# Attention and experts on one core: GpSimd's operations of a pair put beside VectorE's six stretches of maxima

## The chip, the cores and the metric

One Trainium2 chip, one of its cores. The metric is the device time of one execution in microseconds (us); the time of a kernel is the median of its runs. Engines are named as the profile names them: PE is TensorE (PEld its weight loads), DVE is VectorE, ACT is ScalarE, POOL is GpSimd, SP is the engine whose queue issues most transfers.

## What is computed

Attention over 8 batches of 8 heads with pooled queries, and on its output a mixture of 8 experts, one expert for each token:

```python
# attention: q, k, v are (8, 8, 1152, 64)
q_pool = q.reshape(B, H, S // 2, 2, D).mean(axis=3)
scores = scale * q_pool @ k^T
attn = exp(scores - max(scores)) / (sum + 1e-09)
x = attn @ v                                   # 4608 tokens of 512
# experts
logits = x @ w_gate + modality_bias[modality_id]
e = argmax(logits);  g = softmax(logits)[e]
out = g * (relu(x @ w1[e]) @ w2[e])
```

## The kernel before

**Pairs and steps.** The 64 heads go in 32 pairs: head j of two batches lies on partitions 64j to 64j+63. Work on a pair is written as 18 steps (`NSTEP`), and a loop over all steps (line 1250) writes PE's, ACT's, DVE's and POOL's instructions in the order in which they stand in the program; each engine then runs its own in that order and waits for semaphores. SP's transfers are not in this order by hand: a scheduler places them where it expects their data to be ready. Tables of step numbers (`T_SPLIT`, `T_QH`, `T_LO`, `T_HD`, `T_VH`, `T_VL`, `T_VS`, `XL`, lines 41 to 95) say at which step, counted from the pair's first, an operation is written; a negative number lies in earlier pairs' steps, so that while one pair's scores run, the next pairs' operands are made.

**What a step has.** PE makes scores into three PSUM banks (`psc`, lines 990 and 991); ACT turns a bank into exponentials (`Pe`, line 992); the exponential is kept as two float16 parts, the upper half read in place and the lower half (`Pl`) scaled by ACT (line 973, 1152 columns) or by DVE (line 975, 576 columns, uint16 to float16). PE then multiplies both with the values (`xp`, lines 1050 to 1052) into the banks X0 (first head) and X1 (second head). When a head is done, DVE scales its result into `x2` (lines 1068 to 1073); ACT and DVE then split x2 into two float16 parts (`split_x` line 1009, `split_xl` line 1019).

**The maxima.** The softmax's row maxima of a later pair are found from an approximate product of queries and keys (`event`, line 907): six events of a pair, at the steps of `EVENTS` (line 161), that is at 13, 16, 1, 4, 7 and 10 of the running 18 steps. In each, PE writes the banks M0, M1, M2 and, for four of them, X0 or X1 (lines 919 to 933), and DVE reduces them (line 915). Four events have two reductions of 512 columns and one of 1024; the one at step 4 (`rest`) has two small ones, the one at step 13 (`block4`) one of 1024. DVE's lower half of every third step stands just ahead of each event's reductions, so that DVE goes through six stretches in a pair: lower half, maxima, then whatever the tables put behind them, then the next lower half. After the event at step 10 the maxima are gathered (`row`: `m9` line 855, a transpose on PE line 859, `mr` line 868) and a transfer writes `mr` into B2's last row (line 869), which the scores of the next pair need.

**POOL's operations of a pair**, for the pairs from the fourth on (above `HELD`): the pooled sum of the queries (`rawq`, line 700), its float16 copy (`qh`, line 709), the low part of the queries (`lo<-rawq,qh`) and of the keys in two halves (`lo<-rawk,hi`, line 745), the high part of the values in two pieces (`VH`, line 835, 640 and 512 columns), a small copy (`both`, line 814), and the issue of the transfer that loads the keys as float16 (`hi`, line 721). DVE makes the low part of the values in two pieces (`vl`, line 831) and the shifted values (`VS`, line 847).

**Waits set by hand.** `hold(this, until)` (line 659) adds a wait between two instructions; the reason that stands beside it is that the two would share a port. `fast[0]` is the last lower half that was written for DVE. Before, these wait for `fast[0]`: the pooled sum, `lo`'s second index (the first half of the keys) and the second piece of `VH`. `lo`'s first index (the queries) waits for the first `vl` of the pair before it.

**Side work.** After every eighth pair a generator (`route`, line 298) ranks 1152 tokens; it runs a few instructions at a time in the steps of `QUIET`, and its matrix products (lines 353 and 355) take a PSUM bank from `some` (line 642) and wait while `held` says so (line 644).

Of the kernel before, what the change touches and what calls it, by code (L numbers as in the profile page):

```python
# [30 lines left out]
SQ = S // 2  # L31
# [10 lines left out]
HELD = 2  # L42
# [8 lines left out]
LAG = 3  # L51
XL = (6, 5, 3)
LD = 1
# [13 lines left out]
T_KQ = -46  # L67
T_SPLIT = -34
T_QH = -33
T_HI = (-29, -24)  # L70
BY_DMA = 3
T_HD = -33
T_LO = (-23, -26, -17, -19, -26, -17, -23)
T_MAX = -24
# [5 lines left out]
LAG0 = 7  # L80
T_SQ = -20
T_POW = -18
T_VH = (-14, -15)
T_VL = (-11, -2)
T_VS = -12
PARTS = ((0, 5, 9), (0, 5, 9))
# [78 lines left out]
FD = 0  # L165
PD = 0
MANUAL = {ET.PE, ET.Activation, ET.DVE, ET.Pool}
# [444 lines left out]
def attention(tc, ctx, att, ident, npairs, xpool, on_two, on_split, on_scale, jobs, side, set_pm, started, ahead, hip):  # L612
# [28 lines left out]
    bank = lambda: banks[next(turns3)]  # L641
    some = lambda: banks[X0 if now[0] % NSTEP in (13, 14, 15) else M2] if by_events() else bank()
    apart = lambda: banks[M2] if by_events() else bank()
    set_pm(some, lambda: by_events() and now[0] % NSTEP not in (2, 3, 13, 14, 15))

# [10 lines left out]
    st = {p: {} for p in range(npairs)}  # L656
    vl_first, fast = {}, [None]

# [45 lines left out]
    def split_qh(p):  # L704
        s = st[p]
        qh = s["qh"]
        made.add((p, "qh"))
        if p > 1:
            (nc.gpsimd if QH_POOL else nc.vector).tensor_copy(qh, s["q"][:, 0:SQ])
        else:  # L710
            nc.scalar.copy(qh, s["q"][:, 0:SQ])
        for j in range(2):
            r = slice(j * D, (j + 1) * D)
            cols = slice(j * SQ, (j + 1) * SQ) if p < BY_HEADS else slice(4 * P + j * D, 4 * P + (j + 1) * D)
            move(QB[p % 2].rearrange("p u n -> p (u n)")[r, cols], qh[r, cols.start - j * SQ:cols.stop - j * SQ])
# [15 lines left out]
    def split_lo(p, i):  # L731
# [13 lines left out]
        done = (nc.gpsimd if p < 2 or i in LO_POOL else nc.vector).tensor_tensor(o[:, r], t[:, r], h[:, r], op=ALU.subtract)  # L745
        if p > HELD and i < 2:
            hold(done, fast[0] if i else vl_first.pop(p - 1))

# [46 lines left out]
    def power(p):  # L795

        s = st[p]
        pt = some()
        nc.tensor.matmul(pt[:, 0:1], ones.broadcast_to([P, P]), s["ss"], start=True, stop=True)
        later_end(PD if p else 0, lambda: scales(p, pt))  # L800

# [16 lines left out]
    def values(p, i, lo):  # L818
# [8 lines left out]
        if lo and p < 2:  # L827
            nc.gpsimd.tensor_scalar(v, v, s["sc"], None, op0=ALU.mult)
            nc.gpsimd.tensor_tensor(flat(s["vl"][:, c]), v, vh, op=ALU.subtract)
        elif lo:  # L830
            done = nc.vector.scalar_tensor_tensor(flat(s["vl"][:, c]), v, s["sc"], vh, op0=ALU.mult, op1=ALU.subtract)  # L831
            if i == 0:
                vl_first[p] = done
        elif p > 1 and i in VH_POOL:
            done = nc.gpsimd.tensor_scalar(vh, v, s["sc"], None, op0=ALU.mult)  # L835
            if p > HELD and i:
                hold(done, fast[0])
        else:
            nc.scalar.activation(vh, v, AF.Copy, scale=s["sc"])
# [354 lines left out]
    for p in range(npairs):  # L1194
        b = NSTEP * p
        go = lambda t, f, *a, p=p, b=b, **k: at(b + t, p, lambda: f(p, *a), **k)
        if p > 1:
            d = D2 if p == 2 else (0,) * 5
            go(T_K2 - b if p == 2 else T_KQ, load_kq, end=False)
            go(T_SPLIT + d[0], split_q)  # L1200
            go(T_QH + d[1], split_qh)
            if p < BY_DMA:
                for i in range(2):
                    go(T_HI[i] + d[2], split_hi, i)
            else:
                go(T_HD, load_hi)
            for i in range(3 if LOC else 7):
                go(T_LO[LOCI[i] if LOC else i] + d[3], split_lo, i)
            if p < BY_HEADS:
# [6 lines left out]
        elif p:  # L1216
            go(T_P1 - b, place, end=False)
            go(T_M1 - b, lambda p: mxq.append(maxpass(p)), end=False)
            go(T_LV, load_v)
        sq, power_, vh, vs, vl = (T_SQ, T_POW, T_VH, T_VS, T_VL) if p > 1 else V1 if p else V0  # L1220
        if p == 1:
# [547 lines left out]
```

## Time and profile before

| what | value |
|---|---|
| median of 3 runs | 1179.87 us (1179.81 to 1183.86) |
| the profiled execution's own time | 1182.24 us |
| its span, first to last instruction | 1180.5 us |
| mean granted TensorE clock | 0.992 |
| stage of the attention's pairs | from about 30 to 790 us |
| stage of the experts | from about 830 us to the end |

The profile has one execution. Busy time of an engine is the union of its instructions' times in a stretch. In the windows view each row is a stretch of the span with each engine's busy time and instruction count, the granted clock, the busy share of the DMA engines and GB/s. The timeline view has an instruction (or a run of like ones) per row, with the idle time ahead of it in square brackets and what ended that. The chain of waits goes back from the end of a stretch through what released each step.

### The profile page before, as it was taken

The page shows a single profiled execution, that of the slowest core. Times are in us where ns is not written, and L with a number is a line of the kernel's source. Part 1 is how long each engine was busy: PE and PEld are TensorE (multiplying, and loading weights), DVE is VectorE, ACT ScalarE, POOL GpSimd, SP SyncE. Part 2 cuts the span into 40 slices and gives each one's busy share as a digit, 9 for nine tenths or more (in the row PEclk, how much of TensorE's full clock was granted, in tenths as well). Part 3 has the DMA queues.
Part 4 walks back from the last instruction along what each step waited for, and adds up shares of the span by engine and source line. Part 5 has one row for each costly group of instructions (what it writes and reads, how often), then busy time and mean ns, then how long its engine had stood idle before and what let it go on. Part 6 is the DMA issues. An engine that isn't in the chain of part 4 may idle for free.

```text
span 1180.5 us, 36614 instructions
## 1 busy us (share of the span) xinstructions
PE 1100.3 (93%) x15060; PEld 781.2 (66%) x15060; DVE 990.5 (84%) x1730; ACT 894.6 (76%) x1403; POOL 439.1 (37%) x469
## 2 busy tenths in 40 slices
PE   7989898999889989889999998999999999999997
PEld 3766666666666666656666666786676676767665
DVE  6899989999989899979999999988798666675755
ACT  5988888888878888878888888877656566565654
POOL 6754444344443445334443454213223211212111
PEclk8999999999999999989999999999999999999999
DMA  7677868769677696775967766469899999999993
GB/s 218 165 202 179 170 153 184 183 149 203 149 158 175 148 188 162 177 158 134 194 160 180 168 150 147 108 204 294 256 271 267 322 288 280 270 278 274 281 277 118
DMA packets 179696, 237.41 MB, mean 201 GB/s; under 512 B 96479, under 2 KB 127215, under 8 KB 179520
## 3 DMA queue, kind: packets, MB, share of 16 engines
q1 hardware_dynamic: 169254, 206.65, 67.4%
q0 software_dynamic: 10256, 28.33, 11.0%
q8 instruction: 120, 1.97, 0.7%
q14 instruction: 56, 0.46, 0.1%
q10 hardware_dynamic: 10, 0.00, 0.0%
HBM read 163.22 MB, written 18.99 MB: 154 GB/s over the span
## 4 chain that ended last, share of the span: by engine, by line
PE 47%; DVE 37%; DMA 5%; ACT 5%; issue 4%; POOL 2%; POOLq 0%; SPq 0%; DVEq 0%
DVE mp L915 17%; DVE Pl L975 6%; PE po L1531 4%; PE po L1533 4%; PE po L1532 4%; PE ph L1424 4%; PE ph L1426 4%; PE ph L1425 4%; PE psc L991 4%; PE psc L990 4%; DMA B<-mr 4%; PE xp L1050 2%; DVE vl L831 2%; DVE x L1073 2%; DVE x L1019 2%
## 5 line engine op out<-in xcount | busy, mean ns | idle before, releaser
L992 ACT ACTIVATE Pe<-psc 128x432 int32<-128x432 f32 x768 | 383.1, 527 | 112.2 <-PE psc L991 98.1
L1050 PE MATMUL xp<-VH,Pe 128*128 128x65 f16 x2880 | 349.1, 194 | 0.0
L1052 PE MATMUL xp<-VS,Pl 128*128 128x65 f16 x2880 | 346.2, 193 | 0.8 <-DVE Pl L975 0.8
L1051 PE MATMUL xp<-vl,Pe 128*128 128x64 f16 x2880 | 345.6, 192 | 0.0
L1050 PEld LDWEIGHTS <-Pe 128*128 128x128 f16 x2880 | 267.0, 98 | 106.1 <-issue 61.1
L915 DVE TENSOR_REDUCE mp<-pm 128x2 f32<-128x1024 f32 (+3 forms) x319 | 297.1, 939 | 43.4 <-PE pm L933 25.8
L991 PE MATMUL psc<-B 65*128 65x432 f16 (+2 forms) x1152 | 304.4, 288 | 8.7 <-DMA B<-mr 8.6
L990 PE MATMUL psc<-B 128*128 128x432 f16 (+2 forms) x1152 | 305.0, 287 | 1.6 <-ACT Pe L992 0.5
L1051 PEld LDWEIGHTS <-Pe 128*128 128x128 f16 x2880 | 266.5, 98 | 44.7 <-issue 0.4
L1052 PEld LDWEIGHTS <-Pl 128*128 128x128 f16 x2880 | 265.0, 97 | 1.2 <-DVE Pl L975 1.2
L973 ACT ACTIVATE Pl<-Pe 128x1152 f16<-128x1152 uint16 x186 | 216.5, 1164 | 5.9
L1424 PE MATMUL ph<-xpart,w1h 128*128 128x256 f16 x544 | 148.3, 273 | 0.5 <-DVE hl L1430 0.5
L1426 PE MATMUL ph<-xpart,w1l 128*128 128x256 f16 x544 | 148.3, 273 | 0.0
L1425 PE MATMUL ph<-xpart,w1h 128*128 128x256 f16 x544 | 148.3, 273 | 0.0
L975 DVE TENSOR_SCALAR Pl<-Pe 128x576 f16<-128x576 uint16 (+1 forms) x198 | 132.9, 672 | 4.4 <-ACT Pe L992 3.4
L991 PEld LDWEIGHTS <-B 65*128 65x128 f16 x1152 | 113.1, 98 | 11.7 <-issue 1.3
L835 POOL TENSOR_SCALAR VH<-rawv,sc 128x512 f16<-128x512 f32 (+1 forms) x60 | 104.4, 1740 | 42.7 <-PE psc L991 29.1
L990 PEld LDWEIGHTS <-B 128*128 128x128 f16 x1152 | 111.8, 98 | 6.8 <-issue 1.4
L1430 DVE SCALAR_TENSOR_TENSOR hl<-ph,hh 128x512 f16<-128x512 f32 x72 | 49.6, 688 | 75.6 <-ACT hh L1429 75.5
L1531 PE MATMUL po<-w2h,hh 128*128 128x512 f16 x288 | 109.2, 379 | 0.0
L1532 PE MATMUL po<-w2l,hh 128*128 128x512 f16 x288 | 109.2, 379 | 0.0
L1533 PE MATMUL po<-w2h,hl 128*128 128x512 f16 x288 | 109.2, 379 | 0.0
(304 smaller groups left out, 1867.1 us busy)
## 6 DMA issues: line engine op xcount, KB each, us to landing
w2r<-in_w_dram SPq DMA_DIRECT2D x76, 512.0 KB
w1r<-in_w_dram SPq DMA_DIRECT2D x72, 512.0 KB
rawv<-in_att_dram SPq DMA_DIRECT2D x32, 576.0 KB
B<-hi SPq DMA_DIRECT2D x128, 144.0 KB
rawq<-in_att_dram SPq DMA_DIRECT2D x31, 576.0 KB
rawk<-in_att_dram SPq DMA_DIRECT2D x31, 576.0 KB
B<-qh SPq DMA_DIRECT2D x128, 72.0 KB
B<-lo SPq DMA_DIRECT2D x64, 144.0 KB
```

What stands on the lines that cost most here:

```text
L915: most = lambda o, x: nc.vector.tensor_reduce(o, x, op=ALU.max, axis=AX.X)
L973: nc.scalar.activation(low, rest, AF.Copy, scale=LOW)
L975: fast[0] = (nc.vector if eng == 'D' else nc.gpsimd).tensor_single_scalar(low, rest, LOW, op=ALU.mult)
L990: nc.tensor.matmul(o, b1[:, ks], b1[:, qs], start=True, stop=False, skip_group_check=True)
L991: nc.tensor.matmul(o, b2[:, ks], b2[:, qs], start=False, stop=True, skip_group_check=True)
L992: nc.scalar.activation(Pe[:, D + x0:D + x1], pt, AF.Exp, scale=1.0 / 16)
L1050: nc.tensor.matmul(out, Ph[:, qs], vh[:, c, j, 0:D + 1], start=c == 0 and g == 0, stop=False, skip_group_check=True)
L1051: nc.tensor.matmul(out[:, 0:D], Ph[:, qs], vl[:, c, j], start=False, stop=False, skip_group_check=True)
L1052: nc.tensor.matmul(out, Pl[:, qs], vs[:, c, j, 0:D + 1], start=False, stop=c == NKC - 1, skip_group_check=True)
L1424: nc.tensor.matmul(o, hi[:, c, fs], xh[:, :, c], start=c == 0, stop=False)
L1425: nc.tensor.matmul(o, hi[:, c, fs], xl[:, :, c], start=False, stop=False)
L1426: nc.tensor.matmul(o, lo[:, c, fs], xh[:, :, c], start=False, stop=c == 3)
```

## The change

POOL's operations of a pair get new steps: the pooled sum 4 steps earlier and the load of the keys 5 earlier, the queries' copy 2 earlier, the queries' low part 9 earlier, the keys' low part in two stretches in place of one, the two pieces of `VH` swapped and in two stretches. All but the queries' low part, which follows the copy, now wait for `fast[0]`; the wait for the first `vl` is gone. On DVE `vl` moves from step 7 to 16 and from 16 to 1 of the running steps, `VS` from just after the lower half behind `rest` to behind the gathering of the maxima, `split_xl` two steps later, and the three small scale instructions (lines 805 and 807) from ahead of the event at step 1 to ahead of the event at step 4. The side work's matrix products may be written at the steps 13 and 14 alone and then take bank X0; by the order of PE's instructions the third `route`'s products, which went to M2 (`pm_1228`), go to X0 (`xp_107`) now, as those of the first two do in both kernels.

```diff
-XL = (6, 5, 3)
+XL = (8, 5, 3)
...
-T_SPLIT = -34
-T_QH = -33
+T_SPLIT = (-34, -38)
+T_QH = (-33, -35)
...
-T_HD = -33
-T_LO = (-23, -26, -17, -19, -26, -17, -23)
+T_HD = -38
+T_LO = ((-26, -26, -23), (-35, -26, -23))
...
-T_SQ = -20
-T_POW = -18
-T_VH = (-14, -15)
-T_VL = (-11, -2)
-T_VS = -12
+V2 = (-19, -17, (-14, -15), -12, (-11, -2))
+V_EV = (-20, -16, (-11, -14), -7, (-2, 1))
...
-    some = lambda: banks[X0 if now[0] % NSTEP in (13, 14, 15) else M2] if by_events() else bank()
+    some = lambda: banks[X0 if now[0] % NSTEP in (13, 14) else M2] if by_events() else bank()
...
-    set_pm(some, lambda: by_events() and now[0] % NSTEP not in (2, 3, 13, 14, 15))
+    set_pm(some, lambda: by_events() and now[0] % NSTEP not in (13, 14))
...
-            (nc.gpsimd if QH_POOL else nc.vector).tensor_copy(qh, s["q"][:, 0:SQ])
+            done = nc.gpsimd.tensor_copy(qh, s["q"][:, 0:SQ])
+            if p > HELD:
+                hold(done, fast[0])
...
-        if p > HELD and i < 2:
-            hold(done, fast[0] if i else vl_first.pop(p - 1))
+        if p > HELD and i:
+            hold(done, fast[0])
...
-        later_end(PD if p else 0, lambda: scales(p, pt))
+        later_end(1 if p >= BY_HEADS else 0, lambda: scales(p, pt))
...
-            done = nc.vector.scalar_tensor_tensor(flat(s["vl"][:, c]), v, s["sc"], vh, op0=ALU.mult, op1=ALU.subtract)
-            if i == 0:
-                vl_first[p] = done
+            nc.vector.scalar_tensor_tensor(flat(s["vl"][:, c]), v, s["sc"], vh, op0=ALU.mult, op1=ALU.subtract)
...
             done = nc.gpsimd.tensor_scalar(vh, v, s["sc"], None, op0=ALU.mult)
-            if p > HELD and i:
+            if p > HELD:
                 hold(done, fast[0])
...
-        sq, power_, vh, vs, vl = (T_SQ, T_POW, T_VH, T_VS, T_VL) if p > 1 else V1 if p else V0
+        sq, power_, vh, vs, vl = V_EV if p >= BY_HEADS else V2 if p > 1 else V1 if p else V0
```

**DVE, from the lower half behind `rest` to `mr`.** This is the order in which DVE's instructions stand in the middle of a pair, first before (lines of the kernel before):

```order
599 L975 TENSOR_SCALAR Pl_123<-Pe_122 128x576
600 L847 TENSOR_SCALAR VS_129<-VH_128 128x18x64
601 L915 TENSOR_REDUCE mp<-pm_1228 128x1
602 L915 TENSOR_REDUCE mp<-xp_108 128x1
603 L915 TENSOR_REDUCE mp<-pm_1227 128x2
604 L831 SCALAR_TENSOR_TENSOR vl<-rawv,sc,VH_128 128x640
605 L975 TENSOR_SCALAR Pl_125<-Pe_124 128x576
...
609 L855 TENSOR_REDUCE m_8056<-mp 128x9
610 L1019 SCALAR_TENSOR_TENSOR x_7421<-x_7085,sc,x_7420 128x9x64
611 L975 TENSOR_SCALAR Pl_127<-Pe_126 128x576
612 L868 TENSOR_SCALAR mr<-pm_1228 9x128
```

and the same place of the change, whose line numbers are up to four lower:

```order
599 L971 TENSOR_SCALAR Pl_123<-Pe_122 128x576
600 L911 TENSOR_REDUCE mp<-pm_1228 128x1
601 L911 TENSOR_REDUCE mp<-xp_108 128x1
602 L911 TENSOR_REDUCE mp<-pm_1227 128x2
603 L971 TENSOR_SCALAR Pl_125<-Pe_124 128x576
...
607 L851 TENSOR_REDUCE m_8055<-mp 128x9
608 L843 TENSOR_SCALAR VS_129<-VH_128 128x18x64
609 L971 TENSOR_SCALAR Pl_127<-Pe_126 128x576
610 L864 TENSOR_SCALAR mr<-pm_1228 9x128
```

`vl` and `split_xl` have left this part, and `VS` stands behind the gathering `m` in place of `split_xl`.

**DVE, from `mr` to the lower half ahead of the next `rest`**, before:

```order
613 L915 TENSOR_REDUCE mp<-pm_1227 128x2
...
616 L1073 SCALAR_TENSOR_TENSOR x_8148<-xp_107,scales,rr 128x5x64
617 L975 TENSOR_SCALAR Pl_121<-Pe_120 128x576
...
621 L831 SCALAR_TENSOR_TENSOR vl<-rawv,sc,VH_128 128x512
622 L975 TENSOR_SCALAR Pl_123<-Pe_122 128x576
623 L805 TENSOR_SCALAR half<-pm_1228 128x1
```

and now:

```order
611 L911 TENSOR_REDUCE mp<-pm_1227 128x2
...
614 L1069 SCALAR_TENSOR_TENSOR x_8143<-xp_107,scales,rr 128x5x64
615 L1015 SCALAR_TENSOR_TENSOR x_7421<-x_7080,sc,x_7420 128x9x64
616 L971 TENSOR_SCALAR Pl_121<-Pe_120 128x576
...
620 L829 SCALAR_TENSOR_TENSOR vl<-rawv,sc,VH_128 128x640
621 L971 TENSOR_SCALAR Pl_123<-Pe_122 128x576
...
625 L829 SCALAR_TENSOR_TENSOR vl<-rawv,sc,VH_128 128x512
626 L971 TENSOR_SCALAR Pl_125<-Pe_124 128x576
627 L803 TENSOR_SCALAR half<-pm_1228 128x1
```

`split_xl` (now line 1015) and the larger `vl` have come into this part, the smaller `vl` has moved one stretch on in it, and `half` with its two followers stands one stretch later.

**POOL, one pair**, before:

```order
196 L814 COPY both<-scales 64x1
197 L700 TENSOR_TENSOR rawq<-rawq 128x576
198 L835 TENSOR_SCALAR VH_128<-rawv,sc 128x8x64
199 L709 CAST qh<-rawq 128x576
200 L721 DMA hi<-in_att_dram 128x1152
201 L835 TENSOR_SCALAR VH_128<-rawv,sc 128x10x64
202 L745 TENSOR_TENSOR lo<-rawq,qh 128x576
203 L745 TENSOR_TENSOR lo<-rawk,hi 128x576 x2
```

and now:

```order
200 L812 COPY both<-scales 64x1
201 L831 TENSOR_SCALAR VH_128<-rawv,sc 128x8x64
202 L831 TENSOR_SCALAR VH_128<-rawv,sc 128x10x64
203 L743 TENSOR_TENSOR lo<-rawk,hi 128x576 x2
204 L696 TENSOR_TENSOR rawq<-rawq 128x576
205 L719 DMA hi<-in_att_dram 128x1152
206 L705 CAST qh<-rawq 128x576
207 L743 TENSOR_TENSOR lo<-rawq,qh 128x576
```

The two `VH` and the two `lo<-rawk,hi` stand together now, each of the four in a stretch of its own, and the queries' three operations follow behind the keys'.

## Rows read from the trace of the kernel before

**Rows 1.** The page's first part: busy time, share of the span and instructions of each engine.

```profile
PE 1100.3 (93%) x15060; PEld 781.2 (66%) x15060; DVE 990.5 (84%) x1730; ACT 894.6 (76%) x1403; POOL 439.1 (37%) x469
```

**Rows 2.** The windows view by stage: a stretch of the attention and one of the experts. Columns: stretch, length, busy time of each engine, granted clock, DMA share, GB/s.

```profile
400.00:500.00 100.00, 90.93 (x1595) 66.64 (x1593) 92.09 (x166) 85.48 (x142) 43.89 (x43) 1.00 0.75 170
...
900.00:1000.00 100.00, 100.00 (x695) 67.81 (x694) 68.72 (x84) 62.81 (x80) 22.23 (x21) 1.00 0.98 287
```

**Rows 3.** The windows view, cut at DVE's first reduction of `rest` and at the end of the lower half ahead of `mr`: two whole cycles of a pair in four stretches, then the second half of two cycles that hold a `route`. Busy columns in the order PE, PEld, DVE, ACT, POOL.

```profile
388.74:401.73 12.99, 11.46 (x202) 8.25 (x202) 12.35 (x21) 9.89 (x17) 7.90 (x7) 1.00 0.66 169
401.73:412.60 10.87, 10.79 (x194) 7.93 (x192) 9.08 (x19) 10.33 (x18) 2.21 (x3) 1.00 0.46 121
412.60:425.54 12.94, 11.41 (x205) 8.52 (x205) 12.77 (x20) 10.76 (x19) 7.86 (x7) 1.00 0.96 196
425.54:436.46 10.92, 9.71 (x172) 6.97 (x171) 9.02 (x18) 9.81 (x17) 2.13 (x3) 1.00 0.86 179
...
327.99:341.07 13.08, 10.74 (x191) 7.89 (x191) 9.42 (x21) 9.62 (x17) 2.45 (x4) 1.00 0.75 150
...
521.93:537.54 15.61, 13.35 (x190) 9.26 (x190) 9.41 (x20) 9.80 (x17) 2.44 (x4) 0.78 0.56 129
```

**Rows 4.** The timeline of DVE in the second of these cycles (start, duration, line, operation, idle before), with one row of a later cycle at the end.

```profile
412.60 1.42 DVE L915 TENSOR_REDUCE mp<-pm 128x4 f32<-128x512 f32 x2 [0.78 <-PE pm L925]
...
415.18 1.80 DVE L975 TENSOR_SCALAR Pl<-Pe 128x576 f16<-128x576 uint16 x1
416.90 0.44 DVE L847 TENSOR_SCALAR VS<-VH 128x1152 f16<-128x1152 f16 x1
417.36 0.69 DVE L915 TENSOR_REDUCE mp<-pm 128x1 f32<-128x512 f32 x1
...
419.69 0.87 DVE L831 SCALAR_TENSOR_TENSOR vl<-rawv,sc,VH 128x640 f16<-128x640 f32 x1
420.49 0.45 DVE L975 TENSOR_SCALAR Pl<-Pe 128x576 f16<-128x576 uint16 x1
420.85 0.68 DVE L915 TENSOR_REDUCE mp<-pm 128x1 f32<-128x512 f32 x1
...
423.40 1.77 DVE L1019 SCALAR_TENSOR_TENSOR x<-x,sc,x 128x576 f16<-128x576 f32 x1
...
432.03 0.16 DVE L805 TENSOR_SCALAR half<-pm 128x1 int32<-128x1 int32 x1 [0.56 <-PE pm L799]
...
432.93 0.69 DVE L915 TENSOR_REDUCE mp<-pm 128x1 f32<-128x512 f32 x1 [0.49 <-PE pm L933]
...
549.20 0.92 DVE L1019 SCALAR_TENSOR_TENSOR x<-x,sc,x 128x576 f16<-128x576 f32 x1
550.04 0.45 DVE L975 TENSOR_SCALAR Pl<-Pe 128x576 f16<-128x576 uint16 x1
```

**Rows 5.** The timeline of POOL in the same cycle.

```profile
411.99 1.57 POOL L835 TENSOR_SCALAR VH<-rawv,sc 128x512 f16<-128x512 f32 x1 [1.35 <-PE psc L991]
413.51 0.67 POOL L709 CAST qh<-rawq 128x576 f16<-128x576 f32 x1
414.12 0.61 POOL L721 DMA_DIRECT2D hi<-in_att_dram  x1
414.77 1.89 POOL L835 TENSOR_SCALAR VH<-rawv,sc 128x640 f16<-128x640 f32 x1
420.70 1.37 POOL L745 TENSOR_TENSOR lo<-rawq,qh 128x576 f16<-128x576 f32 x1 [4.04 <-issue]
422.05 2.50 POOL L745 TENSOR_TENSOR lo<-rawk,hi 128x576 f16<-128x576 f32 x2
...
432.72 1.40 POOL L700 TENSOR_TENSOR rawq<-rawq 128x576 f32<-128x576 f32 x1
```

**Rows 6.** The groups of DVE's instructions, shapes kept apart, in the stretch from 77.39 to 752.54 us, which is 28 cycles (29 first reductions of `rest`): count, busy time, mean ns of one, idle before and what ended it.

```profile
L975 DVE TENSOR_SCALAR Pl<-Pe 128x576 f16<-128x576 uint16 x168 | 115.5, 688 | 3.2 <-ACT Pe L992 2.4
L915 DVE TENSOR_REDUCE mp<-pm 128x1 f32<-128x512 f32 x112 | 77.2, 689 | 25.6 <-PE pm L933 25.0
...
L1019 DVE SCALAR_TENSOR_TENSOR x<-x,sc,x 128x576 f16<-128x576 f32 x28 | 38.0, 1357 | 0.0
...
L915 DVE TENSOR_REDUCE mp<-pm 128x4 f32<-128x512 f32 x29 | 20.1, 692 | 17.0 <-PE pm L925 17.0
```

**Rows 7.** The chain of waits of the same cycle, in order of time (start, length, what).

```profile
425.17 0.37 DVE Pl L975
425.54 0.21 DVE mr L868
...
425.77 5.24 DMA B<-mr
```

**Rows 8.** The timeline of SP's queue in the same cycle: issues of transfers.

```profile
425.09 0.58 SPq L685 DMA_DIRECT2D rawk<-in_att_dram  x1
425.77 0.80 SPq L869 DMA_DIRECT2D B<-mr  x1
```

**Rows 9.** The timeline of PE where the second `route` has its products.

```profile
524.19 0.22 PE L353 MATMUL xp<-oh,up 128*128 128x72 bf16 x1 [2.62 <-DVE x L1073]
```

**Rows 10.** The page's costliest groups: the two largest of PE in the attention.

```profile
L1050 PE MATMUL xp<-VH,Pe 128*128 128x65 f16 x2880 | 349.1, 194 | 0.0
L1052 PE MATMUL xp<-VS,Pl 128*128 128x65 f16 x2880 | 346.2, 193 | 0.8 <-DVE Pl L975 0.8
```

More of the change, by code (lines that the diff above doesn't have):

```diff
@@ L165 @@
 FD = 0
-PD = 0
 MANUAL = {ET.PE, ET.Activation, ET.DVE, ET.Pool}
@@ L656, in attention @@
     st = {p: {} for p in range(npairs)}
-    vl_first, fast = {}, [None]
+    fast = [None]
     def hold(this, until):
@@ L1199, in attention @@
             go(T_K2 - b if p == 2 else T_KQ, load_kq, end=False)
-            go(T_SPLIT + d[0], split_q)
-            go(T_QH + d[1], split_qh)
+            go(T_SPLIT[p >= BY_HEADS] + d[0], split_q)
+            go(T_QH[p >= BY_HEADS] + d[1], split_qh)
             if p < BY_DMA:
@@ L1206, in attention @@
                 go(T_HD, load_hi)
-            for i in range(3 if LOC else 7):
-                go(T_LO[LOCI[i] if LOC else i] + d[3], split_lo, i)
+            for i in range(3):
+                go(T_LO[p >= BY_HEADS][i] + d[3], split_lo, i)
             if p < BY_HEADS:
```

## The prediction

> **What bounds the kernel now.** I read the page's first part, then the windows by stage, the windows cut inside a cycle, the timelines of DVE and POOL in one cycle, and the chain of waits of that cycle. By the first part PE is busy for 93% of the span, DVE for 84%, ACT for 76% [rows 1]. These are means over two stages: in a stretch of the attention DVE is at 92%, PE at 91%, ACT at 85%, and in the experts PE alone is full [rows 2]. The change touches the attention only. PE's figure there says less than it seems to: a product of 65 columns is drawn 194 ns long, and the groups of lines 1050 and 1052 alone fill 695 us [rows 10], so what is drawn overlaps, and a PE without gaps need not be at its limit.
>
> So I cut the cycle of a pair at DVE's work. Two whole cycles take 47.72 us, 23.86 each [rows 3]. **Part A**, from `rest` to the lower half ahead of `mr`, takes 12.99 and 12.94 us, of which DVE is busy for 12.35 and 12.77 (95 and 99%), ACT for 9.89 and 10.76. **Part B**, from there to the next `rest`, takes 10.87 and 10.92 us, with DVE at 9.08 and 9.02, ACT at 10.33 and 9.81 (95 and 90%) [rows 3]. DVE sets the length of A and ACT that of B; in B, DVE waits for PE three times, 0.56, 0.49 and 0.78 us (the last row is that of the cycle before) [rows 4]. The chain of waits agrees: at the end of A it is on DVE, with the lower half and `mr`, and then on the transfer of `mr` for 5.24 us [rows 7].
>
> In A, DVE is partly blocked, not busy. The lower half takes 0.45 us, but 1.80 us at 415.18 [rows 4], while POOL's `VH` of 640 columns runs from 414.77 for 1.89 us [rows 5]: DVE's instruction ends 0.3 us after POOL's. `split_xl` takes 1.77 us at 423.40 beside POOL's `lo`, 0.92 us at 549.20 [rows 4, 5]. The reductions are not touched: 0.68 us at 420.85 beside `lo` as against 0.69 without POOL at 417.36, and 112 of them have a mean of 689 ns [rows 4 to 6].
>
> **The change, part by part.** Durations in a row of DVE's instructions are taken from start to start.
>
> *Lower half freed.* POOL's operations wait for it now, so it is short: 168 of them have a mean of 688 ns in place of 450, six to a cycle: 1.43 us of a cycle over all, 1.36 in the cycle shown (415.18 to 416.90 as against 420.49 to 420.85) [rows 4, 6]. I take 1.36, all of it in A.
>
> *`split_xl` to B.* It leaves A: 28 of them have a mean of 1357 ns where the free one has 920, so 0.44 of block in the mean; the free one takes 0.84 from start to start (549.20 to 550.04): 1.28 leave A, 0.84 come to B, if POOL is clear of it there [rows 4, 6].
>
> *The larger `vl` to B*: 0.80 us (419.69 to 420.49) [rows 4]. The smaller one and the three scale instructions stay in B, `VS` stays in A; together 0.
>
> *DVE's sums.* A: the mean of 12.35 and 12.77 is 12.56; less 1.36, 1.28 and 0.80 it is 9.12. B: 9.05 and 0.84 and 0.80 make 10.69.
>
> *Lengths.* In A, ACT now has more than DVE: 10.33 (mean of 9.89 and 10.76). The nearest stretch that ACT sets is B of the first cycle, at 95% [rows 3]; so A takes 10.33 / 0.95 = 10.87. B now has DVE above ACT (10.07 in the mean); stretches that DVE sets ran at 95 and 99%; I take the lower end, since DVE still has to meet PE at each event: 10.69 / 0.95 = 11.25. The cycle is 22.12 us, 1.74 less; over the 28 cycles [rows 6] that is 48.7 us.
>
> *The transfer of `mr`.* It is issued behind the load of the keys, 576 KB [rows 8]. In the new order of SP's queue it stands ahead of that load. I cost this at nothing: the gain counts only where the scores wait for it, and A's saving already has `mr` come earlier in the cycle.
>
> *POOL's new places.* Each must fit beside the maxima: 2.4 us from the first reduction to the next instruction (417.36 to 419.69 makes 2.33). The pooled sum and the issue of `hi` are 1.40 + 0.61 = 2.01; `qh` and the queries' `lo` 0.67 + 1.37 = 2.04; `VH` 1.89 and 1.57; each half of the keys' `lo` 1.25 [rows 5]. All fit, `qh` with `lo` by 0.3 us. Behind POOL's waiting operation stand only its own later ones; their readers are transfers for pairs that run a whole cycle later, so I put 0 here. The tightest is `VH` at `rest`, behind the three scale instructions.
>
> *The third `route`.* Its products go to X0, which DVE must have read: the second one waited 2.62 us for that on PE [rows 9]. Cost 2.6 us at most once; from below 0, as the first products there may come late. I take 2.6.
>
> *Sum:* 48.7 less 2.6 is 46.1 us off the profiled execution's 1182.24 us: 1136.1 us. That execution is 2.4 us above the median of 1179.87 us, so I predict **1134 us**.
>
> **A rule weighed.** The rows say that DVE's lower half and `split_xl` block, and that reductions don't. The Trainium skill, SBUF — State Buffer, section Who interferes with whom, says more: a VectorE instruction with two SBUF inputs contends with a GpSimd instruction that reads SBUF, and whoever issues first holds the port for the whole instruction. `split_xl` agrees (1.77 against 0.92 us); for `vl`, which has two SBUF inputs too, no row shows it beside POOL, since the old waits keep them apart. By that rule the new order is exposed where `vl` follows the reductions directly, with 0.3 us to spare.
>
> **The rivals.**
>
> *ACT alone sets the cycle.* A and B lend each other slack; ACT is busy for 20.4 us of a cycle, at 95% 21.5 us. 2.4 us less over 28 cycles is 67, less 2.6: 1115. For it: after the change DVE has 19.8 us, less than ACT. Against: the events tie PE to DVE six times in a cycle.
>
> *PE does not follow.* A's drawn PE time is 11.46 and 11.41 us [rows 3]. If that is real, A falls only to about 11.7; with B at 11.5 the cycle is 23.2, 0.7 less: 18 us less 2.6, 1165. Against it stands the overlap of rows 10.
>
> *The port is blocked elsewhere.* The change doesn't do what it says: POOL starts late by a semaphore's time, `qh` with `lo` reaches into `vl`, `VH` at `rest` into the next lower half. At half of what is blocked now, (1.36 + 0.44) / 2 = 0.9 us of a cycle, 25 us are given back: 1159.
>
> *Slower: B becomes DVE's without its idle time being used.* DVE's 1.83 us of waits in B (0.56, 0.49, 0.78) stay, because PE's event products come in PE's order, and the new 1.64 us are simply added: B is 12.5 us. PE, in order, waits for `half` behind the lower half before it may write M2 for `rest`. A falls only to PE's drawn 11.4. The cycle is 24.0: 4 us more, and with the third `route` and a fall of the clock behind its stall, 9 us: 1189. It decides from the point at which B grows by more than A falls, 1.5 us here. For it: DVE's waits in B are for PE (25.0 and 17.0 us over 28 cycles [rows 6]). Against: ACT is 90 to 95% busy in B, so PE is held by ACT's banks, and DVE's waits are slack. The clock was granted at 1.00 in one cycle with a `route` (13.08 us for B) and 0.78 in the other (15.61 us) [rows 3], part of which then ran at the lower level of 1.2 GHz, so such a stall costs up to 2.5 us more.
>
> **How the numbers follow.** A measurement of this kernel can tell about 0.5% from no change, 6 us. Forecast (1120 to 1150) 0.46; ACT alone (below 1120) 0.17; port blocked elsewhere (about 1159) 0.13; PE doesn't follow (about 1165) 0.14; slower (above 1186) 0.08; no change 0.02. Faster is 0.86, allowing 0.04 of the PE rival to end within 0.5%; same is 0.06, slower 0.08. The range takes in both ends of the forecast (95 or 99% in B, 0 or 2.6 for the third `route`), most of ACT alone and the two smaller gains: 1110 to 1168.
>
> **What would show it.** In the new profile line 971 (the lower half) should have a mean near 450 ns, line 1015 one near 920; A should be near 10.9 us, with ACT as busy as DVE, and B near 11.2 with DVE above 94%. DVE's waits for PE should move from B, 1.83 us of a cycle now, to A. POOL's operations should start at the end of a lower half and end ahead of the next. The forecast is wrong if the mean of line 971 stays above 550 ns, if A stays above 11.5, or if B passes 12.

## The result, and the profile after

The change takes 1137.65 us (median of 4 runs, 1137.29 to 1139.71) where the kernel before takes 1181.3 us beside it: a ratio of 0.9632, 95% interval 0.9608 to 0.9655, 43.7 us off. 1134 us was forecast. The profiled execution is the slowest of the four, 1139.71 us with a span of 1138.0 us, 42.5 us less than that of before. Most of it lies in the 28 cycles between the first and the last `rest`: 675.2 us before (77.39 to 752.54), 629.9 us now (79.41 to 709.35), 45.2 us less. The first `rest` comes 2.0 us later, and what follows the last one takes 0.7 us longer.

The page's first part, which answers to [rows 1], and the shares by engine of the chain that ended last:

```profile
PE 1091.5 (96%) x15060; PEld 778.5 (68%) x15060; DVE 935.3 (82%) x1730; ACT 890.6 (78%) x1403; POOL 436.4 (38%) x469
...
PE 67%; DVE 22%; ACT 7%; DMA 2%; POOL 1%; issue 1%; SPq 0%; POOLq 0%
```

DVE is busy for 55 us less on as many instructions. An instruction of DVE that POOL holds up is drawn as busy all the while, and below such an instruction is called held: the 55 us are time that DVE spent held, not working. Where that was, the groups of DVE's instructions over the 28 cycles show, shapes kept apart, as in [rows 6]:

```profile
L911 DVE TENSOR_REDUCE mp<-pm 128x2 f32<-128x1024 f32 x140 | 170.4, 1217 | 12.4 <-PE pm L915 12.4
L911 DVE TENSOR_REDUCE mp<-pm 128x1 f32<-128x512 f32 x112 | 77.4, 691 | 38.1 <-PE pm L929 37.5
L971 DVE TENSOR_SCALAR Pl<-Pe 128x576 f16<-128x576 uint16 x168 | 76.3, 454 | 3.2 <-ACT Pe L988 2.3
...
L829 DVE SCALAR_TENSOR_TENSOR vl<-rawv,sc,VH 128x640 f16<-128x640 f32 x28 | 24.5, 876 | 0.0
...
L1015 DVE SCALAR_TENSOR_TENSOR x<-x,sc,x 128x576 f16<-128x576 f32 x28 | 22.7, 810 | 0.0
```

The lower half has fallen from 688 to 454 ns and `split_xl` from 1357 to 810 ns, together 54.5 us; `vl` is not held either. The idle time ahead of the small reductions has grown, from 25.6 to 38.1 us: DVE now waits for PE where it used to be held.

Two cycles in the windows view, cut as [rows 3] were (busy time in the order PE, PEld, DVE, ACT, POOL, then granted clock, DMA share, GB/s); the first and third rows are part A, the second and fourth part B:

```profile
348.45:358.58 10.13, 10.00 (x181) 7.43 (x180) 9.04 (x18) 9.10 (x15) 4.83 (x4) 1.00 0.81 223
358.58:370.29 11.71, 11.24 (x197) 8.10 (x195) 10.62 (x21) 11.03 (x20) 5.27 (x6) 1.00 0.85 184
370.29:380.90 10.61, 10.46 (x199) 7.88 (x198) 9.33 (x19) 9.26 (x15) 4.80 (x4) 1.00 0.66 184
380.90:392.61 11.71, 11.24 (x198) 8.10 (x196) 10.62 (x22) 10.99 (x19) 5.27 (x6) 1.00 0.63 151
```

A is 10.4 us in the mean of the two (12.97 before), B 11.71 (10.90 before). DVE is busy for 88 to 89% of A and 91% of B, so it sets neither any more. The timeline of DVE in the first of these cycles:

```profile
351.02 0.46 DVE L971 TENSOR_SCALAR Pl<-Pe 128x576 f16<-128x576 uint16 x1
351.72 0.69 DVE L911 TENSOR_REDUCE mp<-pm 128x1 f32<-128x512 f32 x1 [0.24 <-PE pm L929]
...
354.06 0.45 DVE L971 TENSOR_SCALAR Pl<-Pe 128x576 f16<-128x576 uint16 x1
355.21 0.69 DVE L911 TENSOR_REDUCE mp<-pm 128x1 f32<-128x512 f32 x1 [0.70 <-PE pm L929]
...
359.21 1.22 DVE L911 TENSOR_REDUCE mp<-pm 128x2 f32<-128x1024 f32 x1 [0.44 <-PE pm L915]
...
366.30 0.69 DVE L911 TENSOR_REDUCE mp<-pm 128x1 f32<-128x512 f32 x1 [0.33 <-PE pm L929]
```

and that of POOL, which answers to [rows 5]:

```profile
348.65 1.57 POOL L831 TENSOR_SCALAR VH<-rawv,sc 128x512 f16<-128x512 f32 x1
351.58 1.89 POOL L831 TENSOR_SCALAR VH<-rawv,sc 128x640 f16<-128x640 f32 x1 [1.36 <-DVE Pl L971]
```

POOL's second `VH` starts when the lower half of 351.02 has ended, and ends (353.47) ahead of the next one at 354.06. The chain of waits at the end of B, where [rows 7] had the transfer of `mr` at the end of A:

```profile
366.30 2.42 DVE mp L911 x3
368.72 0.66 DVE vl L829
369.38 0.37 DVE Pl L971
369.75 0.08 DVE half L803
...
369.87 0.38 PE pm L921 x7
```

The transfer has left this part of the chain. PE's wait for it over the whole execution was 8.6 us in the page of before and is 2.5 us now; in the 28 cycles it was 7.4 us and now there is none.

Where DVE's lateness reached PE shows in PE's own waits over the 28 cycles (us in total, times, longest). These are the two largest and that for `mr` before, then one of them in the timeline of PE, then the two largest now:

```profile
PE pm L933 <- DVE mp L915: 13.1, 14, 1.4
PE pm L289 <- DVE mp L915: 11.9, 14, 1.2
...
PE psc L991 <- DMA B<-mr: 7.4, 8, 1.4
```

```profile
419.83 0.59 PE L933 MATMUL pm<-hi,qh 64*128 64x512 f16 x3 [0.83 <-DVE mp L915]
```

```profile
PE pm L921 <- DVE half L803: 9.4, 28, 0.7
PE psc L986 <- ACT Pe L988: 7.1, 27, 0.3
```

Before, PE waited once in each cycle for reductions to be done with a bank; at 419.83 they are the ones that stand behind the lower half held at 415.18. These 25.0 us are gone. All waits that the view names come to 57.1 us before and 23.2 us now.

In their place stands a new step, which is the largest wait now: PE may write M2 for `rest` only when DVE has read `half` out of it, which now comes behind three reductions, `vl` and a lower half.

### The profile page after: what moved, and what is told of

The parts are those of the page before. It is cut to its first block, busy times and chain, and to the rows that moved or that the text cites. A ratio compares the mean times of both kernels' runs of the same rounds, so it can differ in the third digit from the quotient of the medians.

```text
span 1138.0 us, 36590 instructions
## 1 busy us (share of the span) xinstructions
PE 1091.5 (96%) x15060; PEld 778.5 (68%) x15060; DVE 935.3 (82%) x1730; ACT 890.6 (78%) x1403; POOL 436.4 (38%) x469
## 4 chain that ended last, share of the span: by engine, by line
PE 67%; DVE 22%; ACT 7%; DMA 2%; POOL 1%; issue 1%; SPq 0%; POOLq 0%
DVE mp L911 14%; PE psc L986 7%; PE psc L987 7%; PE ph L1420 6%; PE ph L1421 6%; PE ph L1422 6%; PE po L1527 5%; PE po L1528 5%; PE po L1529 5%; PE xp L1046 4%; PE xp L1048 4%; PE xp L1047 4%; PE pm L929 3%; ACT Pl L969 2%; ACT vl L791 2%; DVE vl L829 2%
## 5 line engine op out<-in xcount | busy, mean ns | idle before, releaser
L969 ACT ACTIVATE Pl<-Pe 128x1152 f16<-128x1152 uint16 x186 | 216.5, 1164 | 5.9
L743 POOL TENSOR_TENSOR lo<-rawk,hi 128x576 f16<-128x576 f32 (+1 forms) x68 | 82.8, 1221 | 127.1 <-DVE Pl L971 120.5
L987 PEld LDWEIGHTS <-B 65*128 65x128 f16 x1152 | 113.2, 98 | 20.4 <-issue 11.4
```

The costliest lines, as they stand in the source:

```text
L969: nc.scalar.activation(low, rest, AF.Copy, scale=LOW)
L987: nc.tensor.matmul(o, b2[:, ks], b2[:, qs], start=False, stop=True, skip_group_check=True)
```

## The experiments

The question was which part of the change brings the 44 us, and what keeps it from bringing more. "Block" below is the theory that all of it is DVE's time held behind POOL. Its rivals: DVE's own moves bring the gain by relieving A, or the length is set by ACT or PE. All ratios are to the kernel before; each has an interval of about 0.0025 either way, so that variants less than some 3 us apart are told apart by their traces, not by their times.

| kernel | median us | ratio, 95% interval |
|---|---|---|
| the change | 1137.65 | 0.9632 (0.9608 to 0.9655) |
| pool_new_dve_old | 1132.01 | 0.9580 (0.9550 to 0.9611) |
| pool_old_dve_new | 1174.0 | 0.9935 (0.9908 to 0.9962) |
| no_waits | 1207.44 | 1.0205 (1.0163 to 1.0248) |
| block_back | 1137.5 | 0.9623 (0.9591 to 0.9655) |
| route_m2 | 1128.74 | 0.9557 (0.9538 to 0.9577) |
| start_old | 1134.74 | 0.9610 (0.9591 to 0.9629) |
| vl_later | 1138.56 | 0.9643 (0.9625 to 0.9662) |
| lows_shift | 1138.44 | 0.9651 (0.9629 to 0.9673) |
| xl_back | 1136.99 | 0.9626 (0.9602 to 0.9651) |
| vl_back | 1134.1 | 0.9609 (0.9582 to 0.9635) |
| sc_back | 1133.22 | 0.9588 (0.9564 to 0.9612) |
| best | 1120.99 | 0.9491 (0.9467 to 0.9515) |

**POOL's part alone** (pool_new_dve_old). The change, with DVE's moves undone, but for `VS`, which stands one stretch later than before. The two pieces of `VH`, which come in the same order before and in the change (512 columns, then 640), are swapped here:

```diff
-XL = (8, 5, 3)
+XL = (6, 5, 3)
-V_EV = (-20, -16, (-11, -14), -7, (-2, 1))
+V_EV = (-20, -18, (-14, -11), -8, (-11, -2))
-        later_end(1 if p >= BY_HEADS else 0, lambda: scales(p, pt))
+        later_end(0, lambda: scales(p, pt))
```

> GpSimd's operations are in the six stretches of maxima with their waits, as in the change (the two VH pieces swapped, since the larger vl needs the larger VH early); VectorE's vl, split_xl and the scale instructions are back at the steps of the kernel before, VS one stretch later than there, so all stay in part A. Theory 'block': the gain is the freed lower half and split_xl; A's VectorE work is 12.56 - 1.36 - 0.44 = 10.8 us, A about 11.1, B 10.9, cycle 22.0: within 8 us of the change, 1130 to 1146. Theory 'balance': the gain is the work moved out of A; without it A stays near 12 us, the cycle at 23: about 1160.

It is faster than the change. DVE's groups, then a cycle in its two halves (A, then B) and A of the cycle behind it:

```profile
L971 DVE TENSOR_SCALAR Pl<-Pe 128x576 f16<-128x576 uint16 x162 | 73.8, 456 | 4.1 <-ACT Pe L988 3.3
L1015 DVE SCALAR_TENSOR_TENSOR x<-x,sc,x 128x576 f16<-128x576 f32 x27 | 21.9, 812 | 0.0
```

```profile
142.57:154.28 11.71, 11.55 (x210) 8.45 (x210) 10.86 (x21) 10.14 (x17) 4.07 (x3) 1.00 0.73 226
154.28:164.90 10.62, 10.54 (x189) 7.68 (x186) 9.02 (x18) 10.08 (x17) 6.05 (x7) 1.00 0.70 167
164.90:175.76 10.86, 10.73 (x192) 7.91 (x192) 10.47 (x20) 10.10 (x18) 4.07 (x3) 1.00 0.79 205
```

`split_xl` is as short in A as in B, once POOL keeps clear of it. Cycles of 22.33 and 21.48 us take turns here (B of the second is 10.62 us again), and cycles of 21.84 and 22.32 us in the change. So the gain comes with POOL's new places and waits, which free the lower half, and the 1.64 us of DVE's work that the change moves from A to B bring nothing more. PE's waits in the view above come to 7.3 us here.

How much of the gain is `split_xl`'s isn't shown, and the trace of before speaks against it. There `split_xl` was held in every second cycle only: 1.77 us at 423.40, but in the first cycle of [rows 3]

```profile
400.44 0.92 DVE L1019 SCALAR_TENSOR_TENSOR x<-x,sc,x 128x576 f16<-128x576 f32 x1
```

and A took 12.99 us in that cycle, 12.94 in the one with the hold. Over the 28 cycles the 14 with the hold last 24.08 us in the mean, the 14 without it 24.14. The waits for `mr` too, 7.4 us before, lie only in cycles with the hold.

**DVE's part alone** (pool_old_dve_new). On the kernel before, `vl`, `VS` and `split_xl` in DVE's order of the change; the three scale instructions stay. In short:

```diff
-XL = (6, 5, 3)
+XL = (8, 5, 3)
+V_EV = (-2, 1), -7
...
+        if p >= BY_HEADS:
+            vl, vs = V_EV
...
-            hold(done, fast[0] if i else vl_first.pop(p - 1))
+            hold(done, fast[0] if i else vl_first.pop(p - 1, fast[0]))
```

`vl_first` holds the last reduction of the event at step 7 here, since the first `vl` no longer stands where POOL could wait for it.

> The kernel before with VectorE's vl, VS and split_xl at the new steps and GpSimd's operations where they were (the queries' low part waits for the last reduction ahead of where vl stood). Theory 'block': the lower half is still blocked by VH and now another by lo, each 1 to 1.4 us of a cycle; the mean of the lower half stays above 650 ns and the time is 1165 to 1185. Theory 'balance': A's VectorE work falls to 12.56 - 0.80 - 0.84 = 10.9 us including the block, the cycle to about 22.5: 1140 to 1150.

It gains some 7.5 us, so DVE's moves are worth that much while POOL stays where it was. The block moves instead of going; DVE's groups:

```profile
L976 DVE TENSOR_SCALAR Pl<-Pe 128x576 f16<-128x576 uint16 x152 | 119.0, 783 | 3.0 <-ACT Pe L993 2.2
L846 DVE TENSOR_SCALAR VS<-VH 128x1152 f16<-128x1152 f16 x25 | 24.2, 967 | 0.0
L1020 DVE SCALAR_TENSOR_TENSOR x<-x,sc,x 128x576 f16<-128x576 f32 x25 | 20.2, 809 | 0.0
```

`split_xl` is free, but the lower half has risen from 688 to 783 ns and `VS`, 0.44 us in [rows 4], takes 0.97.

**POOL's new order without its waits** (no_waits):

```diff
     def hold(this, until):
+        return
```

> The change with no wait between GpSimd's operations and a lower half at all; the steps are the change's. If the places alone do it: mean of the lower half under 480 ns and 1136 to 1140. If the waits are needed: GpSimd starts as soon as its data are there, reaches into lower halves, their mean is 550 to 700 ns; in the 'block' theory 10 to 35 us slower than the change (1148 to 1172).

It is slower than the kernel before by 2%, which I had not expected. POOL runs through its operations as soon as it can. The timelines of POOL and DVE at one place, and the row of PE's wait for `mr` (2.5 us in the change):

```profile
406.03 3.43 POOL L832 TENSOR_SCALAR VH<-rawv,sc 128x512 f16<-128x512 f32 x2
409.44 2.51 POOL L744 TENSOR_TENSOR lo<-rawk,hi 128x576 f16<-128x576 f32 x2
411.91 1.39 POOL L697 TENSOR_TENSOR rawq<-rawq 128x576 f32<-128x576 f32 x1
```

```profile
409.60 4.02 DVE L972 TENSOR_SCALAR Pl<-Pe 128x576 f16<-128x576 uint16 x1
```

```profile
L988 PE MATMUL psc<-B 65*128 65x432 f16 (+2 forms) x1152 | 316.5, 297 | 45.8 <-DMA B<-mr 45.8
```

One lower half, begun 0.16 us behind POOL's first `lo`, is held through three operations, to 0.3 us after the last of them ends at 413.30. And the scores wait 45.8 us for `mr`: in the cycle of 393.30 its transfer takes 6.74 us, in a stretch whose DMA share is 1.16 (the profiled execution is the slowest of this kernel's):

```profile
392.77:400.03 7.26, 4.75 (x88) 3.33 (x85) 6.73 (x13) 5.76 (x10) 0.00 (x0) 1.00 1.16 215
400.03:407.03 7.00, 6.94 (x96) 4.93 (x96) 3.73 (x8) 4.62 (x8) 1.16 (x2) 0.76 0.97 177
```

After that stall the granted clock was 0.76, so part of the stretch ran at 1.2 GHz. The waits thus do more than keep POOL off the lower half: with them PE hardly waits for `mr`. That they do it by spreading the transfers that POOL's results release is what this one stretch suggests; it isn't shown for the others, and 8.1 of the 45.8 us are a single wait ahead of the first `rest`.

**The block put back** (block_back). The two `VH` directly behind one another, the second across a lower half:

```diff
-V_EV = (-20, -16, (-11, -14), -7, (-2, 1))
+V_EV = (-20, -16, (-14, -14), -7, (-2, 1))
```

> The change with both VH pieces written in the one stretch of rest, as in the kernel before, so that the second reaches into the next lower half: one block of 1 to 1.4 us of a cycle is restored, in part A, and all else stays. If VectorE sets A still (block theory): the cycle grows by about 1 us, 28 us more: 1165. If A is now set by ScalarE with VectorE at 9.2 of 10.4 us: most of it is hidden, 0 to 8 us more: 1138 to 1146.

The time is that of the change, and the experiment did not make what it was to measure: the lower half starts inside the second `VH` and isn't held.

```profile
348.12 3.43 POOL L831 TENSOR_SCALAR VH<-rawv,sc 128x640 f16<-128x640 f32 x2
```

```profile
350.49 0.50 DVE L971 TENSOR_SCALAR Pl<-Pe 128x576 f16<-128x576 uint16 x1
```

It says nothing for or against the theory, so no run puts the block back by itself; what it shows of the chip stands in the last section.

**The side work's products in M2** (route_m2), at all steps:

```diff
-    some = lambda: banks[X0 if now[0] % NSTEP in (13, 14) else M2] if by_events() else bank()
+    some = lambda: banks[M2] if by_events() else bank()
```

> The change with the side work's products at the steps 13 and 14 in bank M2, which no event holds then, in place of X0. If the three waits of 2.0 us for VectorE's reading of X0 (and what the clock loses behind them) are paid in full: 5 to 9 us less, 1129 to 1133. If they are hidden or come back as another wait: 1136 to 1139.

8.9 us less than the change. Part B of the three cycles with a `route`, in the change, and PE's wait in the last of them:

```profile
311.01:326.13 15.12, 13.08 (x208) 9.07 (x206) 10.95 (x23) 11.37 (x20) 5.56 (x7) 0.89 0.88 199
491.65:505.62 13.97, 11.66 (x208) 8.44 (x206) 10.95 (x23) 11.30 (x20) 5.55 (x7) 1.00 0.99 216
672.33:686.67 14.34, 11.84 (x213) 8.61 (x211) 11.53 (x27) 11.67 (x20) 5.76 (x7) 1.00 0.65 130
```

```profile
675.12 0.19 PE L349 MATMUL xp<-oh,up 128*128 128x72 bf16 x1 [1.83 <-DVE x L1069]
```

and in route_m2:

```profile
308.82:320.79 11.97, 11.58 (x208) 8.45 (x206) 10.84 (x23) 11.18 (x20) 5.57 (x7) 1.00 0.94 223
486.29:498.27 11.98, 11.59 (x208) 8.45 (x206) 10.85 (x24) 11.18 (x20) 5.56 (x7) 1.00 0.98 206
664.98:677.31 12.33, 11.74 (x213) 8.61 (x211) 11.43 (x25) 11.54 (x20) 5.78 (x7) 1.00 0.77 151
```

Each stall costs 2.0 us of the cycle in full, and 3.2 where the granted clock fell to 0.89: 7.2 us of the 8.9. The rest lies ahead of the first `rest`, where executions differ by as much without this edit (next experiment).

**The start** (start_old). The fourth pair's operations of POOL at their steps of before; the new steps from the fifth on:

```diff
-            go(T_SPLIT[p >= BY_HEADS] + d[0], split_q)
+            go(T_SPLIT[p > BY_HEADS] + d[0], split_q)
```

and likewise for `qh`, the load of `hi` and `lo`.

> The change with the first of the pairs concerned (the fourth) at the steps of the kernel before for its pooled sum, copy, low parts and load, all later pairs as changed. If GpSimd's earlier work for that pair holds up VH of the third, VS waits 2.4 us for it, PE runs dry and its clock falls: 2 to 4 us less than the change, 1134 to 1136. If the start has other reasons: 1136 to 1139.

2.9 us less, as much as the resolution. In the change, POOL does the fourth pair's queries ahead of the third pair's `VH`; `VS` waits 2.37 us for that (1.70 in the kernel before), then PE, whose clock falls behind the gap. The row of `VS` in the change and in start_old, and a window of the change:

```profile
55.89 0.46 DVE L843 TENSOR_SCALAR VS<-VH 128x1152 f16<-128x1152 f16 x1 [2.37 <-POOL VH L831]
```

```profile
54.44 0.45 DVE L843 TENSOR_SCALAR VS<-VH 128x1152 f16<-128x1152 f16 x1
```

```profile
60.00:64.00 4.00, 4.00 (x53) 3.01 (x51) 2.81 (x6) 1.51 (x3) 1.28 (x1) 0.66 1.03 384
```

The wait is gone, and the stretch around it, between two reductions of DVE's line 895, is 2.0 us shorter (48.87 to 59.74 us, in the change 48.30 to 61.19). More isn't shown. The first `rest` comes at 76.25 us in place of 79.41, but in the eight other variants that keep the change's start, with `VS` waiting 2.36 or 2.37 us in each, it comes anywhere from 75.82 to 80.74: the clock fell behind the gap in two of them and stayed at 1.00 in six.

**What keeps the cycle at 22 us.** Two kernels, each with one edit on the change. In vl_later the smaller `vl` stands a stretch later, so that `half` is read sooner; in lows_shift, 144 columns of every lower half go from ACT to DVE:

```diff
-V_EV = (-20, -16, (-11, -14), -7, (-2, 1))
+V_EV = (-20, -16, (-11, -14), -7, (-2, 7))
```

```diff
-LOWS = (((0, 1152, 'A', 2), (1152, 1728, 'D', 3)), ((0, 1152, 'A', 2), (1152, 1728, 'D', 3)))
+LOWS = (((0, 1008, 'A', 2), (1008, 1728, 'D', 3)), ((0, 1008, 'A', 2), (1008, 1728, 'D', 3)))
```

> The change with the smaller vl at step 7 of the running steps in place of 1: 0.66 us leave the stretch ahead of half, for whose read of M2 PE waits before rest, and go to part A. If that chain over VectorE sets B: cycle 0.4 to 0.6 us shorter, 1120 to 1127. If ScalarE sets the cycle: 0 to 3 us less.

> The change with 144 of the 1152 columns of each lower half that ScalarE makes given to VectorE (1008 and 720): ScalarE 0.8 us of a cycle less, VectorE 0.55 us more. If ScalarE's work sets the cycle: 0.4 to 0.8 us less, 1116 to 1127. If VectorE or its chain through the events sets it: 0 to 15 us more.

Neither moves the time. In vl_later PE's wait for `half`, 9.4 us over the 28 cycles of the change, is gone and a wait for `vl` has come; the largest of PE's waits there:

```profile
PE xp L1047 <- DVE vl L829: 10.9, 27, 0.7
```

In lows_shift ACT's part of the lower half fell from 1164 to 1044 ns a piece, about 0.7 us of a cycle, and nothing came of it: ACT's amount of work doesn't set the cycle by itself. DVE took on 0.44 us of a cycle for it (528 ns a piece), and PE's wait for `half` grew from 9.4 to 12.9 us while that for ACT's `Pe`, 7.1 us, went; so ACT's share isn't separated by this run.

**Which of DVE's moves costs.** One move undone in each: `split_xl` (xl_back), `vl`, `VS` and the scales (vl_back), or the scales with the power ahead of them alone (sc_back):

```diff
-XL = (8, 5, 3)
+XL = (6, 5, 3)
```

```diff
-V_EV = (-20, -16, (-11, -14), -7, (-2, 1))
+V_EV = (-20, -18, (-11, -14), -7, (-2, 1))
-        later_end(1 if p >= BY_HEADS else 0, lambda: scales(p, pt))
+        later_end(0, lambda: scales(p, pt))
```

(this is sc_back; vl_back is the first experiment without its first edit, so that `VS` and the pieces of `VH` stand as there).

> The change with split_xl alone back in the first half of the cycle. The measured first half is 0.5 us shorter and the second 0.5 us longer than forecast, so the theory 'split_xl is the move that costs' (0.84 us of DVE's path from the longer half to the shorter) expects 1131 to 1134 us here, and 1136 to 1139 in the run with vl, VS and the scales back. The rival 'the cost is the wait of PE for half, or vl in the second half' expects 1136 to 1139 us here.

> The change with both vl, VS and the three scale instructions at their old places, split_xl moved as in the change. Theory 'split_xl is the move that costs': 1136 to 1139 us. Rival 'vl or the scales cost': 1131 to 1134 us. If both runs gain about half (1134 to 1136), the cost is that of DVE's sum in the second half, whatever the operation.

> The change with the three scale instructions (and the power ahead of them) alone back, one stretch earlier, so that PE need not wait for half ahead of rest. Theory 'the wait for half costs' (up to 0.47 us of a cycle, 13 us at most): 1131 to 1134 us. Theory 'split_xl or vl costs', or that another wait takes its place, as happened when the smaller vl went a stretch later: 1136 to 1139 us.

1137.0, 1134.1 and 1133.2 us: `split_xl` costs nothing that can be told, the scales 4.4 of the 5.6 us (each within some 3 us). The theory that `split_xl` costs fell. Part B in sc_back, where `half` is read a stretch earlier:

```profile
156.63:168.10 11.47, 11.39 (x198) 8.16 (x196) 10.60 (x20) 10.71 (x18) 5.36 (x7) 1.00 0.66 155
```

It is 0.24 us shorter than the 11.71 above, with DVE's work the same. PE's waits agree: those for `half` come to 9.4 us in the change and 8.9 in xl_back, but to 2.1 in sc_back and 1.0 in vl_back, and the 7.1 us for ACT's `Pe` go with them. With vl_later this says: it is the read of `half` that counts, as long as no other operand of PE becomes late for it.

**The three together** (best): pool_new_dve_old with the edits of route_m2 and start_old.

> The change with GpSimd's new places and waits alone (VectorE's moves undone), the side work's products always in M2, and the fourth pair's operations at their old steps. If the three gains lie at different places they add: 1132.0 - 8.9 - 2.9, about 1120 us (1118 to 1123). Rival: they share their slack (the undone moves and the route both free PE in the second half of a cycle): 1124 to 1129 us, no better than the route's edit alone.

1120.99 us, a ratio of 0.9491 (0.9467 to 0.9515), 16.7 us below the change. The three gains add in the medians (1132.0 − 8.9 − 2.9 makes 1120.2), but without the start's the sum is 1123.1, which the interval (1118.2 to 1123.9 us) takes in too. The traces show the `route`'s: the 28 cycles take 616.6 us here and 625.3 in pool_new_dve_old. `VS` doesn't wait at the start here either, yet the first `rest` comes at 77.14 us, against 77.28 there; that the start's gain adds isn't shown. PE's waits in the 28 cycles come to 1.2 us: PE hardly waits for another engine there.

## Why the prediction was right, step by step

*Lower half freed: right.* 115.5 − 76.3 us over 28 cycles is 1.40 us of a cycle; 1.36 was taken. With it went the 25.0 us that PE waited for reductions, and POOL's part alone has the whole gain without DVE's moves. The hold taken away is 39.2 us and the cycles' gain 45.2, but no run frees the lower half alone, and what the rest is was not separated.

*`split_xl` and `vl` to B, clear of POOL: right in the durations* (810 and 876 ns), *wrong in what they are worth.* The step took them as relief of A, `split_xl` with a mean of 1357 ns. That mean mixes 14 of 1.77 us with 14 of 0.93, and A was as long with the one as with the other, since DVE waited in the A with the free one (busy for 12.35 of 12.99 us). So DVE's sum did not set every A, as the step had it. DVE's sums came out as worked out, 9.04 and 9.33 in A (9.12) and 10.62 in B (10.69), but pool_new_dve_old has the same cycle, or a shorter one, without the moves.

*Lengths: the sum was right, the split was not.* The step that failed is "A set by ACT at 10.33, B by DVE at 95%". It took ACT's work as fixed to a half. ACT's sum of a cycle stayed (20.40 us before, 20.19 now), but about 1 us of it went from A to B, which the step had no reason to rule out: the cut is at DVE's instructions, and ACT's are not tied to it. So A is 10.4 us, not 10.87, and B 11.71, not 11.25; together 22.08, where 22.12 was forecast. As neither bound holds, that the two errors of half a microsecond cancel is in part luck. DVE has 91% of B where over 94% was forecast, and ACT, with 94%, is no bound by itself either, by lows_shift. What sets 22 us is left open in part: PE, in its order, waits for one engine and then another (for `half`, for a bank that ACT reads), and one wait taken away can uncover the next, as in vl_later. In pool_new_dve_old and best, where hardly a wait is left in the 28 cycles (7.3 and 1.2 us), what remains is PE's own time as drawn, of which the traces don't tell how near it is to its limit. DVE's waits for PE moved as forecast, though only in part: 0.94 us in A (351.72 and 355.21) and 0.99 in B (0.44 and 0.33 above, and 0.22 ahead of `rest`).

*Over 28 cycles:* 48.7 less 2.6 was forecast, 45.2 us was measured. In the mean the cycles were longer than the ones I took, by 0.25 us before (24.11 against 23.86) and by 0.29 after (22.50 against 22.21 with the `route`'s part). That this cancels is in part luck: the three cycles with a `route` are part of both means, and what they cost depends on the clock.

*The transfer of `mr` at nothing: borne out as far as the traces go.* PE's waits for it in the 28 cycles fell from 7.4 us to none, but before, the cycles that had them were no longer than the others.

*POOL's new places fit: right in the cycles, wrong at the start*, which no step looked at: 2.0 us by the stretch around `VS` in start_old. The steps of the fourth pair reach back beyond the stretch for which the new order was drawn.

*The third `route`, 2.6 us: right in size* (2.0 us of a cycle, and more where the clock falls). The step missed that the first two stalls were there to be had as well.

*The moved scale instructions at nothing: wrong by 4.4 us.* The prediction has the cost in its slower rival (PE waits for `half`) and not in its sum.

The rivals: "the port is blocked elsewhere" fell with the means of lines 971, 829 and 1015, and the rule weighed for `vl` was not met, since in the 28 cycles of the change none began inside one of POOL's operations of a pair; "PE does not follow" with A at 10.1 to 10.6 us, below PE's drawn 11.4 of before; "ACT alone", with its 1115 us, by the measured time; the slower one with B below 12 outside the three cycles with a `route`. Its wait of PE for `half` did come, though.

## What to carry to other kernels

Where an instruction's mean is well over its shortest time, look for what ran beside it, and price the held time before anything else: here most of the gain goes with the freed lower half, and moving work of the same engine between two stretches was then worth nothing or less. Look at the single instructions behind the mean as well: where some are held and some are not, the stretches that hold them show whether the hold costs time. Before a small instruction is moved because it is short, ask which other engine may not go on until it has run: reading `half` a stretch later cost some 4 us, the move of `split_xl` none. And a wait between two engines also sets when transfers start, so taking waits out can make a small transfer late. And compare the start of several executions before a gain there is believed.

## What the runs showed of the hardware that was not expected

*What holds a lower half.* Among lower halves and `VS` that began with over 0.45 us of a POOL instruction still to run, beside `lo` (two inputs) all 64 were held, in before, pool_old_dve_new and no_waits, at any point from 0.04 to 0.80 us into it. Beside `VH` (one input) 26 of 27 were held in the kernel before, begun 0.01 to 0.86 us into it, but only 2 of 30 in block_back and 4 of 22 in no_waits, where that `VH` nearly always follows another directly. In these two they sort by where they began: in block_back none was held up to 0.82 us into the `VH` and both from 0.95 us on, in no_waits none up to 1.01 us and all from 1.11 us on. The Trainium skill, SBUF — State Buffer, section Who interferes with whom, has whoever issues first hold the shared port for the whole instruction. The rows of `lo` and those of before agree; those of block_back and no_waits would agree only if such a `VH` took the port later than its span is drawn to begin, which no run shows by itself. Why they differ is open; POOL's spans in a trace are rough.

*Held through several instructions.* In no_waits a waiting DVE instruction did not come in between two of POOL's: it took 4.02 us, through three of them.
